# Attention with beacon keys, then a maxout FFN: batch 0 divided at query 512, and the first two batches in a new order

## The chip, the cores and the metric

The kernel runs on one core of a Trainium2 chip. The metric is the device time of one execution in microseconds (us). A core has a matrix engine (TensorE, PE in the profile; its weight loads are PEld), a vector engine (VectorE, DVE), an engine for functions and copies (ScalarE, ACT), a general engine (GpSimd, POOL) and a queue engine (SyncE, SP). Each works through its own instructions in order; they wait for one another by semaphores. Transfers between the main memory and the on-chip memory (SBUF) are DMAs, issued here by SP, ACT and POOL. Matrix products are accumulated in PSUM, a small memory of eight banks of 512 fp32 columns.

## The reference

Inputs are q, k and v (8 batches, 8 heads, 576 positions, 64 features), 16 beacon keys and values per head, three input weights (512 x 768) and an output weight (768 x 512), all fp32. Per batch and head:

```python
k_all = concatenate([beacon_k, k]); v_all = concatenate([beacon_v, v])   # 592 keys
scores = q @ k_all.T / sqrt(64)          # causal among the 576; beacons seen by all
a = exp(scores - max); a /= sum(a)
x = a @ v_all                            # then heads side by side: 4608 tokens x 512
h = maximum(maximum(x @ w1, x @ w2), x @ w3)
out = h @ w_out                          # 4608 x 512
```

## The kernel before, in words

Work is cut into 16 quads: quad Q is batch Q // 2 and four of its eight heads. For a quad the four heads lie on four groups of 32 partitions, and each pair of features is one 32-bit word. q and k come in (fp32 for quads 0 and 1, cast in a separate instruction; bf16 by a casting DMA of POOL for all later ones), and VectorE turns them with 32 x 32 transposes of words into `qT` and `kT` (`turn`, L197 to L205). The beacon keys go through `turn_first_beacon_k` (L160) or `turn_beacon_k` (L148) and `put_beacon_k` (L167).

Keys are in five tiles of up to 128, tile 0 beginning with the 16 beacons. Tile t needs only queries from `q_min[t]` on (0, 112, 240, 368, 496), so a quad has 576 + 464 + 336 + 208 + 80 = 1664 columns of scores per head. They are cut into steps of at most 512 columns (`bursts`, L69 to L87): four steps of their own shape for each of quads 0 to 3, and full 512-column steps running across quads from quad 4 on. A step (`emit_scores`, L258) is a run of small matmuls into two PSUM tiles of two heads each, then two exponentials on ScalarE (L288), one per tile, which write bf16 probabilities to `at_sb`; no maximum is subtracted. `emit_masks` (L298) zeroes the causal triangle with POOL selects (L304).

The division by the sum comes afterwards. For quads 0 to 3 `pv_pass` (L316) makes, for each half of the queries (288), three passes: part 0 multiplies the probabilities by ones and gets the sums, from which ScalarE makes a logarithm (L344) and an exponential of its negative (L346), that is the reciprocal; parts 1 and 2 multiply by the even and odd columns of v, and VectorE multiplies PSUM by the reciprocal into `xT` (L350). From quad 4 on `pv_segment` (L357) does the three parts together, for queries 0 to 239 and then 240 to 575. `xT` is a ring of four batches, already transposed for the FFN.

The FFN runs in nine blocks of 512 tokens. A block is 18 first-layer units (`mm1_unit`, L427: four 512-column matmuls; the first of three results is copied to `hT`, by ScalarE, or for block 0 by VectorE at L447, the others are joined by a maximum on VectorE, L449) and four second-layer units (`mm2_unit`, L451: six matmuls, a copy, an output DMA). Units are taken strictly in order, and one may start when the last batch that its tokens reach is complete (`ready`). Block 0 takes all of w1 first, then w2, then w3.

The order is written by hand (`tc.manual_schedule()`): every engine executes what `emit_all` (L606) emits, in that order. `begin` (L544) starts 17 multiplications of zeros (`spare`, L538) and the first loads: SP issues the k of quad 0 in two pieces, its q in two, the k and q of quad 1 (L183), beacon keys, v of batch 0 (L218) and the small beacon loads. Then come the steps in order. Around them stand probability passes, `heads` (transposes between a step's two exponentials), FFN units up to a running allowance (2 per step in steps 8 to 15, then 2.6 and 3.4), and `plan`, work tied to a step (`at_step`, L565 to L579): the loads of later quads and of the weights on POOL's queue, the casts of v, the transposes. FFN units begin behind step 8, when both quads of batch 0 have been divided. After the last step the rest of the units run.

```python
N_APART = 2 * n_quad
by_burst = [
    [[(0, 0, HALF), (3, q_min[3], S)], [(1, q_min[1], S)], [(2, q_min[2], S)]]
    + [[(0, HALF, S), (4, q_min[4], S)]],
    [[(t, q_min[t], S) for t in range(n_kt)]],
]
```

Of the kernel before, what the change touches and what calls it, by code (L numbers as in the profile page):

```python
# [16 lines left out]
def kernel(  # L17
# [27 lines left out]
    HG = 4  # L45
# [15 lines left out]

    BANK = 512
    N_APART = 2 * n_quad
    by_burst = [
        [[(0, 0, HALF), (3, q_min[3], S)], [(1, q_min[1], S)], [(2, q_min[2], S)]]
        + [[(0, HALF, S), (4, q_min[4], S)]],
        [[(t, q_min[t], S) for t in range(n_kt)]],
    ]
    bursts = []  # L69
    at_piece = {}  # L70
    for Q in range(NQ):
        apart = Q < N_APART
        pos = 0
        if Q <= N_APART:
            room = 0
        for group in by_burst[0 if apart else 1]:
            if apart:
                room = 0
            for t, q0, q1 in group:
                at_piece.setdefault((Q, t), []).append((q0, q1, pos))  # L80
# [7 lines left out]
    AT_W = pos  # L88
# [4 lines left out]
    RING = 4  # L93
# [8 lines left out]
    st_pool = ctx.enter_context(tc.tile_pool(name="st", bufs=4))  # L102
    vst_pool = ctx.enter_context(tc.tile_pool(name="vst", bufs=2))
# [3 lines left out]
    nrm_pool = ctx.enter_context(tc.tile_pool(name="nrm", bufs=2))  # L107
    ffn_h = ctx.enter_context(tc.tile_pool(name="ffn_h", bufs=2))
# [29 lines left out]
    for x in first32:  # L138
        nc.gpsimd.memset(x, 0.0)
# [38 lines left out]
    def load_qk(Q, which, cuts):  # L178
        st = st_pool.tile([128, QS * D], FP32, name="st")
        stage[Q, which] = st  # L180
        for s0, s1 in zip(cuts, cuts[1:]):
            cols = slice(s0 * D, s1 * D)
            nc.sync.dma_start(out=st[:, cols], in_=qk_rows(Q, which)[:, cols])  # L183
# [5 lines left out]
    def cast_qk(Q, which, cast, s0=0, s1=QS):  # L189
# [4 lines left out]
        if s1 == QS:  # L194
            stage.pop((Q, which))

    def turn(Q, which, s0=0, s1=QS):  # L197
# [6 lines left out]
        if s1 == QS:  # L204
            stage.pop((Q, which, 16))  # L205
# [3 lines left out]
    def load_v(b, queue=None):  # L209
        queue = queue or nc.sync  # L210
# [3 lines left out]
        for t in range(n_kt):  # L214
# [43 lines left out]
    def emit_scores(k):  # L258
# [6 lines left out]
        for heads in ((0, 1), (2, 3)) if burst[0][0] < n_quad else (range(HG),):  # L265
# [50 lines left out]
    def pv_pass(Q, hf, part):  # L316
        b, g = divmod(Q, n_quad)
        at_sb, v_sb = at[Q], v_tiles[b]
        h0, h1 = hf * HALF, (hf + 1) * HALF
# [6 lines left out]
        ps = pv_pool[0].tile([128, HALF], FP32, name="pv")  # L326
# [15 lines left out]
        if part == 0:  # L342
            lnd = nrm_pool.tile([128, S - SPLIT], FP32, name="lnd")[:, 0:HALF]
            nc.scalar.activation(out=lnd, in_=ps, func=AF.Ln)  # L344
            recip = nrm_pool.tile([128, S - SPLIT], FP32, name="recip")[:, 0:HALF]
            nc.scalar.activation(out=recip, in_=lnd, func=AF.Exp, scale=-1.0)  # L346
            recips[Q, hf] = recip
        else:
            c0 = b % RING * S + h0
            nc.vector.tensor_mul(xT[:, 2 * g + part - 1, c0 : c0 + HALF], ps, recips[Q, hf])  # L350
# [6 lines left out]
    def pv_segment(Q, seg):  # L357
# [8 lines left out]
        pv_banks = pv_pool[1].tile([128, 2 * BANK], FP32, name="pv2")  # L366
# [28 lines left out]
        recip = nrm_pool.tile([128, S - SPLIT], FP32, name="recip")[:, 0:n]  # L395
# [13 lines left out]

    def pv_pairs(Q):  # L410
        if Q >= N_APART:
            return [[(Q, 0)], [(Q, 1)]]
        return [
            [(Q, 0, 0), (Q, 1, 0)],
            [(Q, 0, 1), (Q, 0, 2)],
            [(Q, 1, 1), (Q, 1, 2)],
        ]

    def emit_pv(passes):
        if len(passes) == 1:  # L420
            return pv_segment(*passes[0])
        for one in passes:
            pv_pass(*one)

    hTs = {}

    def mm1_unit(tb, ft, i, pool, name):  # L427
# [15 lines left out]
        if i == 0 and tb > 0:  # L443
            nc.scalar.copy(hT[:, ft, :], ps)  # L444
        elif i == 0:

            nc.vector.tensor_copy(hT[:, ft, :], ps)  # L447
        else:
            nc.vector.tensor_max(hT[:, ft, :], hT[:, ft, :], ps)  # L449
# [68 lines left out]

    plan = {}
# [199 lines left out]
```

## Time and profile before

| what | value |
|---|---|
| median of 3 runs (lowest, highest) | 287.39 us (287.2, 287.74) |
| the profiled execution, its span | 287.24 us, 285.5 us |
| busy: PE, DVE, ACT, POOL | 272.4, 171.2, 157.5, 88.9 us |
| mean granted PE clock over the span | 0.981 |
| first FFN weight load | 29.36 us into the span |
| first scores of quad 4 (step 16) | 54.44 us |
| DMA, moved and mean rate | 33.08 MB, 116 GB/s |

The span is the time from the first to the last profiled instruction of the program. Busy time of an engine is the union of its instructions; matmuls overlap in a pipeline, so a PE that counts as busy may still be waiting in part. In the lines shown below, "x16" counts instructions, what stands behind "<-" in brackets is what ended the idle time ahead of them, and a name ending in q (SPq, POOLq) is an engine's instruction queue. The 40 slices of the page are each a fortieth of the span, about 7.1 us, and a digit is a tenth.

### The profile page before, as it was taken

The numbers are of one execution on the slowest core, as the hardware profiler recorded it, in microseconds if no ns is written. First come the engines' busy times: TensorE is split into PE (matmuls) and PEld (weight loads), VectorE is DVE, ScalarE is ACT, GpSimd is POOL, SyncE is SP. The second block draws the span as 40 slices with busy tenths as digits, with TensorE's granted clock in tenths as the row PEclk, the third lists the DMA queues.
The fourth block names the chain that finished last, engine by engine and source line by source line (L and its number), as shares of the span: only waits on it lengthen the run. The fifth ranks groups of instructions, "written<-read, shape, count | busy, mean of one in ns | idle before, by whom it ended". The sixth has DMA issues, their size and how long they took to land.

```text
span 285.5 us, 8144 instructions
## 1 busy us (share of the span) xinstructions
PE 272.4 (95%) x3469; PEld 140.2 (49%) x3503; DVE 171.2 (60%) x298; ACT 157.5 (55%) x246; POOL 88.9 (31%) x165
## 2 busy tenths in 40 slices
PE   7597999999999999999999999999999999999995
PEld 2235444534545454445456877445454554444442
DVE  3717769856675766656657575666544454554553
ACT  5798576457784766557664686376647620210210
POOL 0484862235553523152415340442134100000000
PEclk9859999999999999999999999999999999999999
DMA  7899999689964954159046913490031003003004
GB/s 246 226 181 209 144 186 205 94 151 238 203 114 123 218 103 84 48 164 195 5 83 197 203 22 69 152 170 2 2 112 39 2 0 131 18 0 147 3 0 147
DMA packets 51924, 33.08 MB, mean 116 GB/s; under 512 B 41264, under 2 KB 42288, under 8 KB 51888
## 3 DMA queue, kind: packets, MB, share of 16 engines
q1 hardware_dynamic: 41152, 20.40, 27.0%
q0 software_dynamic: 10464, 12.01, 26.5%
q8 instruction: 27, 0.44, 0.6%
q10 hardware_dynamic: 272, 0.15, 0.2%
q14 instruction: 9, 0.07, 0.1%
HBM read 35.13 MB, written 9.44 MB: 156 GB/s over the span
## 4 chain that ended last, share of the span: by engine, by line
PE 90%; ACT 4%; DMA 2%; DVE 1%; issue 1%; SPq 0%; DVEq 0%
PE fps L436 37%; PE fps L456 11%; PE sc L273 11%; PE pv L385 10%; PE pv L436 7%; PE sc L436 6%; ACT at_sb L288 3%; PE pv L334 3%; PE sc L456 2%; PE pv L456 2%; DMA st<-in_q_dram 2%; DVE qT L200 1%; DVE xT L350 0%; ACT recip L346 0%; SPq L183 0%
## 5 line engine op out<-in xcount | busy, mean ns | idle before, releaser
L288 ACT ACTIVATE at_sb<-sc 128x1024 bf16<-128x1024 f32 (+7 forms) x128 | 104.0, 861 | 31.8 <-PE sc L273 31.5
L436 PE MATMUL fps<-xT,w_sb 128*128 128x512 bf16 (+1 forms) x507 | 115.0, 358 | 2.2 <-issue 1.3
L436 PEld LDWEIGHTS <-w_sb 128*128 128x128 bf16 x720 | 66.9, 98 | 68.8 <-issue 7.2
L304 POOL TENSOR_SCALAR_AFFINE_SELECT at_sb<-at_sb 128x512 bf16<-128x512 bf16 (+6 forms) x89 | 48.0, 556 | 126.9 <-ACT at_sb L288 121.8
L449 DVE TENSOR_TENSOR hT<-hT,fps 128x512 bf16<-128x512 bf16 x80 | 54.7, 685 | 33.2 <-PE fps L436 27.3
L273 PE MATMUL sc<-qT,kT 32*128 32x288 bf16 (+15 forms) x960 | 40.1, 266 | 4.5 <-DVE qT L200 2.1
L444 ACT CAST hT<-fps 128x512 bf16<-128x512 f32 x34 | 19.9, 586 | 30.1 <-PE fps L436 30.1
L401 DVE TENSOR_TENSOR xT<-pv,recip 128x240 bf16<-128x240 f32 (+1 forms) x48 | 19.7, 453 | 28.0 <-ACT recip L396 27.5
L456 PE MATMUL fps<-w_out_sb,hT 128*128 128x512 bf16 x144 | 34.9, 379 | 0.5 <-issue 0.3
L456 PEld LDWEIGHTS <-hT 128*128 128x128 bf16 x210 | 19.8, 98 | 25.4 <-DVE hT L449 1.7
L273 PEld LDWEIGHTS <-kT 32*128 32x128 bf16 x960 | 19.1, 94 | 24.1 <-issue 18.0
L394 ACT ACTIVATE lnd<-pv 128x240 f32<-128x240 f32 (+1 forms) x24 | 9.9, 412 | 31.1 <-PE pv L385 31.0
L464 DVE COPY y<-fps 128x512 f32<-128x512 f32 x25 | 17.3, 692 | 12.6 <-PE fps L456 12.2
L200 DVE STREAM_TRANSPOSE kT<-c 128x256 uint32<-128x256 uint32 (+1 forms) x32 | 22.0, 708 | 3.5 <-ACT c L193 3.5
L436 PE MATMUL pv<-xT,w_sb 128*128 128x512 bf16 (+1 forms) x107 | 22.4, 339 | 0.1
L200 DVE STREAM_TRANSPOSE qT<-c 128x256 uint32<-128x256 uint32 (+1 forms) x32 | 21.5, 701 | 0.3 <-ACT c L193 0.3
L385 PE MATMUL pv<-at_sb,v_sb 128*32 128x160 bf16 (+7 forms) x864 | 21.5, 242 | 0.0
L436 PE MATMUL sc<-xT,w_sb 128*128 128x512 bf16 x78 | 20.3, 379 | 0.1
L385 PEld LDWEIGHTS <-v_sb 128*32 128x32 bf16 (+1 forms) x864 | 16.3, 96 | 1.3
L226 POOL CAST v_sb<-vst 128x1024 bf16<-128x1024 f32 (+1 forms) x18 | 15.7, 894 | 0.8 <-issue 0.8
L449 DVE TENSOR_TENSOR hT<-hT,pv 128x512 bf16<-128x512 bf16 x15 | 10.3, 688 | 7.6 <-PE pv L436 4.1
L449 DVE TENSOR_TENSOR hT<-hT,sc 128x512 bf16<-128x512 bf16 x13 | 8.9, 688 | 7.4 <-PE sc L436 5.5
(50 smaller groups left out, 146.9 us busy)
## 6 DMA issues: line engine op xcount, KB each, us to landing
out_dram<-y SPq DMA_DIRECT2D x35, 256.0 KB, 2.0
vst<-in_v_dram SPq DMA_DIRECT2D x21, 256.0 KB, 5.2
c<-in_k_dram POOLq DMA_DIRECT2D x14, 288.0 KB, 5.4
c<-in_q_dram POOLq DMA_DIRECT2D x14, 288.0 KB, 6.7
w_sb<-in_moe_w_dram POOLq DMA_DIRECT2D x3, 768.0 KB, 8.4
vst<-in_v_dram SPq DMA_DIRECT2D x7, 224.0 KB, 3.9
vst<-in_v_dram SPq DMA_DIRECT2D x7, 160.0 KB, 7.6
w_out_sb<-in_moe_w_out_dram POOLq DMA_DIRECT2D x1, 768.0 KB, 9.6
```

The source lines that it names most:

```text
L200: nc.vector.transpose(dst.rearrange("p (t s) -> p s t", s=RUN)[:, s0:s1], src.rearrange("p (s d) -> p s d", d=DP),)
L226: cast(v_tiles[b][0:n, t0:t1].rearrange("p t h d -> p (t h d)"), stage["v", b][0:n, t0:t1].rearrange("p t h d -> p (t h d)"),)
L273: nc.tensor.matmul(sc[h // 2][:, h % 2, off : off + w], kT[hs, 128 * t : 128 * (t + 1), j], qT[hs, q0:q1, j], start=(j == 0), stop=(j == 1 ...
L288: nc.scalar.activation(out=at[Q][:, 2 * i : 2 * i + 2, a0 : a0 + w], in_=sc[i][:, :, off : off + w], func=AF.Exp, scale=scale,)
L304: nc.gpsimd.affine_select(out=view, in_=view, compare_op=ALU.is_ge, fill=0.0, base=q0 - (128 * t - Nb), pattern=[[0, HG], [1, edge - q0]], ...
L385: nc.tensor.matmul(pv_banks[32 * j : 32 * j + 32, c : c + w], lhsT, at_sb[0:r, j, a : a + w], start=(t == 0), stop=all(x[1] // BANK != c / ...
L401: nc.vector.tensor_mul(xT[:, 2 * g + part - 1, c0 : c0 + n], pv_banks[:, offs[part] : offs[part] + n], recip,)
L436: nc.tensor.matmul(ps[:, o0 : o0 + n], w_in[i][:, ct, 128 * ft : 128 * (ft + 1)], xT[:, ct, x0 : x0 + n], start=(ct == 0), stop=(ct == n_c ...
L444: nc.scalar.copy(hT[:, ft, :], ps)
L449: nc.vector.tensor_max(hT[:, ft, :], hT[:, ft, :], ps)
L456: nc.tensor.matmul(ps, hT[:, ft, 128 * tt : 128 * (tt + 1)], w_out_sb[:, ft, :], start=(ft == 0), stop=(ft == n_ft - 1),)
L464: nc.vector.tensor_copy(y, ps)
```

## The change

1. The score steps of the first two quads. Queries 0 to 511 of batch 0 (`main`) are made first, in three steps per quad (0 to 5); then queries 512 to 575 of both quads (`rest`), and then quads 2 and 3 whole, run together in full steps (6 to 13). Quad 4 begins at step 14. There are 53 steps in place of 55.
2. Dividing. `pv_pass` of batch 0 covers queries 0 to 287 and 288 to 511. The remaining 64 queries of both quads are done by one `pv_rest`: 120 matmuls of 64 columns into one bank, one logarithm, one exponential, two multiplies. Quads 2 and 3 use `pv_segment`. Block 0 of the FFN, tokens 0 to 511, thus needs only the main part.
3. Loads of quad 0. q and k come in halves of 288 tokens, each in four DMAs, one per head on 32 partitions (`load_half`): the first k half from SP and ACT, the first q half from SP, ACT and POOL, the second k half from SP, the second q half as bf16 from POOL (`load_half16`). The beacon keys of quad 0 are issued by POOL instead of ACT. The first k half is cast by VectorE, the first q half by POOL, the second k half by ScalarE. The memory for them is cleared by VectorE instead of POOL.
4. Zeros. 30 multiplications of 256 columns in place of 17 of 512 before the first scores, and 36 more of them between the early steps.
5. The order. `plan` and the allowance of the early steps give way to one list, `orders`, walked up to step 13. In it S is a step with its first exponential, E the second exponential and the masks, s, p, r, g and h are probability work, C casts, t transposes, B and b beacon keys, k, w, v loads, c casts of v, x zeros, f one FFN unit (with 1, its copy by VectorE; with 2, in the pool of the probability passes). By step 14, 21 units have been emitted and quads 0 to 3 are divided.
6. Later. The rate is 3.2 units per step in place of 3.4, `xT` holds all eight batches, the reciprocals have a pool of four, v's staging has one buffer, and the very last `pv_segment` uses a score tile instead of the one that the segment ahead of it uses.

The core of the diff:

```diff
+    main = [[(0, 0, HALF), (1, q_min[1], HALF)]]
+    main.append([(2, q_min[2], HALF), (0, HALF, TOKB), (1, HALF, TOKB)])
+    main.append([(2, HALF, TOKB), (3, q_min[3], TOKB), (4, q_min[4], TOKB)])
+    rest = [[(t, TOKB, S) for t in range(n_kt)]]
+    whole = [[(t, q_min[t], S) for t in range(n_kt)]]
...
+    order = [(Q, main) for Q in range(n_quad)] + [(Q, rest) for Q in range(n_quad)]
+    order += [(Q, whole) for Q in range(n_quad, NQ)]
...
-    RING = 4
+    RING = B
...
+    def load_half(which, half, queues):
+        st = half_pool.tile([128, HRUN * D], FP32, name="half32")
+        stage[0, which, half] = st
+        for h in range(HG):
+            src = (q, k)[which][0, h, HALF * half : HALF * (half + 1)]
+            queues[h % len(queues)].dma_start(
+                out=st[32 * h : 32 * h + 32], in_=src.rearrange("(p s) d -> p (s d)", s=HRUN)
+            )
...
+    def pv_rest():
+        n_r = S - TOKB
+        bank = pv_pool[0].tile([128, 512], FP32, name="pv")
+        ps = bank[:, 0 : 3 * n_quad * n_r].rearrange("p (g c n) -> p g c n", g=n_quad, c=3)
+        for part in range(3):
+            for Q in range(n_quad):
+                for t in range(n_kt):
+                    a = next(a + TOKB - q0 for q0, q1, a in at_piece[Q, t] if q0 <= TOKB < q1)
...
+                        nc.tensor.matmul(
+                            ps[32 * j : 32 * j + 32, Q, part],
+                            lhsT,
+                            at[Q][0:n, j, a : a + n_r],
...
+        for part in (1, 2):
+            nc.vector.tensor_mul(
+                xT[:, part - 1 : n_ct : 2, TOKB:S], ps[:, :, part], recip
+            )
...
     def spare(n):
-
         ps = ffn_psum.tile([128, TOKB], FP32, name="fps")
         for _ in range(n):
-            nc.tensor.matmul(ps, zeros[:, 0:128], zeros, start=True, stop=True)
+            nc.tensor.matmul(ps[:, 0:256], zeros[:, 0:128], zeros[:, 0:256], start=True, stop=True)
...
     def begin():
-        spare(17)
-        load_first_beacon_k(0, nc.scalar)
-        load_qk(0, 1, (0, SH, QS))
-        load_qk(0, 0, (0, SH, QS))
-        load_qk(1, 1, (0, QS))
-        load_qk(1, 0, (0, QS))
+        load_half(1, 0, (nc.sync, nc.scalar))
+        load_half(0, 0, (nc.sync, nc.scalar, nc.sync, nc.gpsimd))
+        load_first_beacon_k(0, nc.gpsimd)
+        load_half16(0, 1)
+        load_half(1, 1, (nc.sync,))
+        load_qk(1, 1)
         load_first_beacon_k(1, nc.sync)
+        load_qk(1, 0)
         load_v(0)
         load_beacon_k(1, 2, nc.sync)
+        load_beacon_k(2, B, nc.sync)
...
+        orders = (
+            "C 0 1 1 0; C 0 0 0 2; C 0 1 0 1; t 0 1 0; B 0; t 0 0 0; x 29; k 2 0; x 1; t 0 1 1; t 0 0 "
+            "1; S 0; C 1 0 2 2; x 4; E 0; S 1; x 3; x 2; B 1; x 4; C 1 1 2 1; t 1 1 0; x 4; t 1 1 1; "
+            "E 1; t 1 0 0; x 2; S 2; E 2; t 1 0 1; k 2 1; w 0; c 0 2; x 6; s 0 0; t 2 0 0; S 3; x 6; "
+            "x 3; E 3; S 4; E 4; x 2; c 2 4; c 4 5; s 0 1; p 0 1 1; S 5; p 0 0 2; p 0 1 2; k 3 1; E "
+            "5; v 1 0 1; s 1 0; w 1; k 3 0; p 0 0 1; b 2; v 1 1 2; S 6; b 3; p 1 0 2; p 1 0 1; s 1 1; "
+            "t 2 1 1; p 1 1 1; E 6; v 1 2 3; p 1 1 2; t 2 0 1; f; f 2; t 2 1 0; t 3 1 1; S 7; b 4; f "
+            "1; E 7; f 2; r; w 2; f 1 2; v 1 3 4; S 8; t 3 0 1; t 3 0 0; E 8; f 1; v 1 4 5; f; f 1 2; "
+            "S 9; f 2; E 9; t 3 1 0; f; w 3; g 2 0; S 10; f 1; E 10; h 2 0; f; f 1; S 11; E 11; f 1; "
+            "f 1; f 1; k 5 1; k 4 0; S 12; E 12; g 2 1; k 4 1; S 13; E 13; h 2 1; f; f; k 5 0; g 3 0; "
+            "t 4 0 1; t 4 0 0; h 3 0; f; t 4 1 1; f; g 3 1; t 4 1 0; f; h 3 1 "
+        )
...
-        first_rate, rate = 2.6, 3.4
+        first_rate, rate = 2.6, 3.2
...
+        first, second = segs
+        emit_ffn(len(units), B - 2)
+        finish = pv_segment(*first)
+        banks = sc_psum.tile([128, 2, BANK], FP32, name="sc").rearrange("p a n -> p (a n)")
+        finish_second = pv_segment(*second, banks)
+        finish()
+        finish_second()
+        emit_ffn(len(units), B - 2)
```

334 lines of the change are left out of this document (186 added, 148 removed).

## The prediction

> **What bounds the kernel now.** I read the page's slices first, then the stages, then the order of time in the first stage.
>
> ```profile
> PE 272.4 (95%) x3469; PEld 140.2 (49%) x3503; DVE 171.2 (60%) x298; ACT 157.5 (55%) x246; POOL 88.9 (31%) x165
> PE   7597999999999999999999999999999999999995
> PEclk9859999999999999999999999999999999999999
> DMA  7899999689964954159046913490031003003004
> ```
>
> TensorE (PE) is the bound from the fifth slice on; only the first four, some 28 us, are in question, and there the granted clock dips as well. The stages:
>
> ```profile
> 8.00:16.00 8.00, 5.68 (x56) 2.28 (x56) 4.89 (x11) 6.58 (x8) 4.75 (x7) 0.73 0.91 201
> 16.00:24.00 8.00, 7.44 (x123) 3.70 (x123) 3.21 (x8) 7.54 (x12) 6.17 (x10) 0.63 1.06 189
> 24.00:32.00 8.00, 6.38 (x157) 3.90 (x145) 5.69 (x12) 4.00 (x8) 4.18 (x7) 1.00 1.17 191
> ```
>
> The columns are PE, PEld, DVE, ACT, POOL busy, granted clock, DMA share, GB/s. From 8 to 24 us ScalarE (ACT) is the full engine (6.58 and 7.54 of 8 us), and PE's "busy" there is scores waiting on it. In order of time:
>
> ```profile
> 0.81 0.84 SPq L183 DMA_DIRECT2D st<-in_k_dram  x2
> 1.48 5.46 PE L542 MATMUL fps<-zeros 128*128 128x512 bf16 x17 [1.48 <-DVE zeros L536]
> 4.78 0.33 SPq L183 DMA_DIRECT2D st<-in_q_dram  x1
> 5.22 2.03 SPq L158 DMA_DIRECT2D first<-in_beacon_k_dram  x4
> 9.19 6.79 ACT L288 ACTIVATE at_sb<-sc 128x992 bf16<-128x992 f32 x8 [1.66 <-PE sc L273]
> 10.81 1.14 POOL L193 CAST c<-st 128x1152 bf16<-128x1152 f32 x1 [9.77 <-DMA st<-in_q_dram]
> 16.23 1.89 ACT L288 ACTIVATE at_sb<-sc 128x992 bf16<-128x992 f32 x2 [0.26 <-PE sc L273]
> 19.06 1.58 PE L334 MATMUL pv<-at_sb,ones 128*32 128x288 bf16 x32
> 20.01 0.41 ACT L344 ACTIVATE lnd<-pv 128x288 f32<-128x288 f32 x1
> 20.45 0.45 ACT L346 ACTIVATE recip<-lnd 128x288 f32<-128x288 f32 x1
> 21.57 2.76 ACT L288 ACTIVATE at_sb<-sc 128x672 bf16<-128x672 f32 x4
> 21.99 0.82 DVE L350 TENSOR_TENSOR xT<-pv,recip 128x288 bf16<-128x288 f32 x2 [4.72 <-PE pv L334]
> 29.25 1.17 POOL L304 TENSOR_SCALAR_AFFINE_SELECT at_sb<-at_sb 128x448 bf16<-128x448 bf16 x2 [3.82 <-ACT at_sb L288]
> 29.36 1.41 PEld L436 LDWEIGHTS <-w_sb 128*128 128x128 bf16 x8
> 31.82 1.78 ACT L288 ACTIVATE at_sb<-sc 128x928 bf16<-128x928 f32 x2 [2.63 <-PE sc L273]
> ```
>
> Exponentials of quads 0 and 1 run from 9.19 to 24.33; the first FFN unit stands at 29.36, because it needs all of batch 0. I call that moment F. From F on PE is full:
>
> ```profile
> 40.54 0.90 PE L334 MATMUL pv<-at_sb,ones 128*32 128x288 bf16 x32
> 43.72 0.63 PE L334 MATMUL pv<-at_sb,v_sb 128*32 128x288 bf16 x24
> 46.62 1.18 PE L334 MATMUL pv<-at_sb,v_sb 128*32 128x288 bf16 x40
> 54.44 0.63 PE L273 MATMUL sc<-qT,kT 32*128 32x512 bf16 x8
> 57.70 0.64 PE L273 MATMUL sc<-qT,kT 32*128 32x64 bf16 x16
> ```
> ```profile
> 85.96 1.80 PE pv L385 x76
> 91.02 1.29 PE pv L456 x6
> 93.85 0.86 PE pv L436 x4
> 95.58 0.65 PE pv L385 x24
> ```
> ```profile
> 62.00:231.00 169.00, 166.76 (x2522) 90.84 (x2529) 102.94 (x175) 108.54 (x173) 59.54 (x111) 1.00 0.50 111
> ```
>
> Between F and 54.44 (quad 4's first scores) lie 18 first-layer units of 0.86, seven score steps of about 0.6 and two quads of probability passes (0.90 + 0.63 + 1.18, twice): 15.6 + 4.2 + 5.4 = 25.2, against 25.1 passed. So PE work after F is paid at its own length, and the later stage (166.76 of 169 us) leaves nothing to win. What the change can move is F, and what PE does just behind it.
>
> **The change, part by part.** The sum is made against the profiled execution: 287.24 us, of which 285.5 are span and 1.7 lie around it; the median of the runs is 0.15 above.
>
> *Work dropped from before F.* With token block 0 needing queries 0 to 511 only, quads 0 and 1 want 1344 of their 1664 score columns before F, so ACT does 2 x 2 x 2 x 320 = 2560 columns fewer there: at 1.78 per 2 x 928, 2.5 us. But step 6 (the first of the rest) stands ahead of the last sums in ACT's order with one of its two tiles, 1.0 back.
>
> *The start.* Quad 0 needs only two half loads before its first scores, so these come earlier than 8.54. What holds them is POOL: its cast of the q half stands behind nine DMA issues at about 0.55 (row below), so free at 0.8 + 5.0 = 5.8; cast 0.6, transpose 0.7, scores near 7.3. I bank nothing: the next quad decides.
>
> ```profile
> 36.06 0.58 POOL L187 DMA_DIRECT2D c<-in_k_dram  x1
> st<-in_k_dram SPq DMA_DIRECT2D x1, 576.0 KB, 4.9
> st<-in_q_dram SPq DMA_DIRECT2D x1, 576.0 KB, 6.0
> DMA to landing us min/median/max: 4.0/6.4/11.3
> DMA to landing us min/median/max: 7.9/8.4/10.2
> ```
>
> (The last two are the bf16 q and k loads, L187, and the weights, L249.) Quad 1's q was the sixth issue of SP, at 4.78, and landed at 10.8. Now 13 issues precede it: 9 x 0.42 + 4 x 0.51 + 0.81 = 6.6. With a landing of 4.9 to 6.0 it is there at 11.5 to 12.6; I take 12.1.
>
> *The chain to F.* POOL casts that q (1.14: 13.25), and only behind it come the masks of steps 0 and 1 (1.17 + 0.3: 14.7). The sums of quad 0 wait for those masks, and step 3's scores are queued behind the sums on PE: 0.35 for PE, 0.41 + 0.45 on ACT: 15.95. Then ACT's order is step 3 (1.78), step 4 (1.89), logarithm and reciprocal (0.67), step 5 (1.47), again (0.86), the half of step 6 (1.0), again (0.67): 8.4; seven hand-overs at about 0.15, with 0.26 the one seen, add 1.0: 25.35. Two multiplies of 224 columns (0.82 for two of 288) give F = 26.0, 3.4 earlier.
>
> *Behind F.* Up to quad 4's first scores (step 14) PE now does 18 units of 0.86, 3 second-layer units of 1.29, seven score steps at 0.6, quads 2 and 3 by segments (2 x (0.65 + 1.80) = 4.9, before 5.4), and the rest of batch 0: 120 narrow matmuls. Narrow ones cost by columns (16 with 64 and 448 columns took 0.64, 8 of 512 took 0.63), so 30 groups of four at 64 columns are 1.2. Sum 15.5 + 3.9 + 4.2 + 4.9 + 1.2 = 29.7; step 14 at 55.7. Before, the same state (quads 0 to 3, 21 units) is 54.44 + 3.9 = 58.3. Gain 2.6. All that follows is the same work: 39 score steps, 12 quads, 177 units. The rates 3.4 to 3.2 only move units into the last stage; zero on a full PE. The last segment in its own banks removes at most the 0.4 of one hand-over; I take 0.
>
> *New waits behind F.* Weights and quad 4's loads are issued by POOL behind masks. w1 goes out near 25.0 (step 5's masks end at 23.6, two v issues) and is wanted by the seventh unit, at 26.0 + 5.2 + 1.2 + 1.2 = 33.6; landing 7.9 to 10.2 means 32.9 to 35.2. A wait of 0 to 1.6, and for all loads 0 to 4 (below); nearest is w1's median, no wait, and I take 0.4 over all of them.
>
> *Zeros.* 30 of half width before the scores replace 17 of full width (5.46), so end near 6.2, ahead of the scores. 36 more stand between the early steps, 0.1 each, in time that PE spends waiting on ACT: nothing; without that cover 3.6 us, spread over five gaps, of which the wait for quad 1 alone covers most.
>
> What they may buy is the clock: 32 sums took 1.58 at 19.06 in a stage of granted 0.63, and 0.90 later. [...]
>
> Sum: 287.24 - 2.6 + 0.4 = 285.0, beside the median 285.1.
>
> **Rivals.** *Earlier still.* If quad 1's q is there by about 10.8 as before and ACT never pauses, it needs from 8.0: 5.1 for steps 0 to 2, 0.86, 8.4, the multiplies 0.7 and 0.3 of hand-overs, F = 23.4, 2.6 better: 282.4. For it: ACT was nearly gapless in 9 to 24 us. Against: thirteen issues ahead, and masks behind the cast.
>
> *The start gains nothing.* Quad 1 waits for bytes. Before, 2.36 MB took until 10.8, 3.8 us per MB from 1.8; now quad 2's q (0.59 MB) is requested ahead of quad 1's, 13.0; if q lands 2.5 us past my value, at 14.6, F is 28.5 and the time 287.2. For it: a DMA share of 0.91 already in 8 to 16 us. [...] Against: this chain has few bytes more than before.
>
> *Slower: quad 4's loads late.* Before they were issued at 36.06, 18 us ahead of use. Now q4 is issued behind step 11's masks, near 45.5, and k4 behind step 12's, near 47; their transposes stand on DVE between PSUM evacuations, so a late load stops the FFN too, and step 14 wants them at 55.7. With 6.4 to landing k4 is turned by 54.9: hidden. With 11.3 it is 59.8: a wait of 4.1 on PE, no gain left from 9.9 on, and the time 287.24 - 2.6 + 4.1 = 288.7. For it: the DMA is full (0.9 and more) through 50 us in the slices above. Against: the weights, most of that traffic, are through by 47.
>
> **How the numbers follow.** Forecast 0.48 (own range 283.6 to 286.7); earlier still 0.14; gains nothing 0.14; slower 0.24. A measurement of this kernel tells about 0.2%, 0.57 us, from no change. Faster: 0.48 + 0.14 = 0.62; same 0.14; slower 0.24. Range 282.4 to 288.7, the outer rivals' times.
>
> **What would show it.** Right: first FFN weights load near 26; granted clock 1.0 through 8 to 24 us; POOL's cast of quad 1's q starting near 12.1; step 14's scores near 56; no PE wait over 1 us between. Wrong: that cast past 14; PE waiting on w1 near 33, or on a transpose of quad 4 past 50; the stage from 60 to 230 longer than before; zeros found on the chain between scores.

## The result: slower, and where the profile says so

The changed kernel takes 296.52 us (median of six runs, 294.83 to 296.85), the kernel before, on the same chip, 287.49. The ratio is 1.0291, with an interval of 1.0268 to 1.0313. The forecast was 285.1 with a range of 282.4 to 288.7; the time lies outside it.

The page of the changed kernel, profiled at 296.37 us, first the span, then busy times and the slices:

```profile
span 294.7 us, 8667 instructions
PE 274.7 (93%) x3715; PEld 141.5 (48%) x3752; DVE 168.7 (57%) x300; ACT 157.6 (53%) x250; POOL 94.9 (32%) x178
PE   7647979999989899999999999999999999999995
PEclk9989799999999999999999999999999999999999
DMA  6959997975970979531955494128012002102003
```

PE's busy time has grown by 2.3 us, the span by 9.2. From the seventh slice on PE is full nearly throughout, so the loss is early again. The stages (columns as in the prediction: PE, PEld, DVE, ACT, POOL busy, granted clock, DMA share, GB/s):

```profile
8.00:16.00 8.00, 5.14 (x89) 3.86 (x88) 3.72 (x8) 5.59 (x7) 0.09 (x1) 1.00 0.94 201
16.00:24.00 8.00, 5.42 (x95) 3.35 (x98) 3.37 (x6) 3.42 (x5) 6.86 (x11) 0.79 0.68 132
24.00:32.00 8.00, 5.65 (x217) 4.69 (x209) 3.63 (x10) 4.97 (x11) 5.72 (x11) 0.86 1.12 181
```

From 16 to 24 us ACT, the full engine of this stage before (7.54 of 8 us), works 3.42. POOL does next to nothing before 16 (0.09, before 4.75) and is nearly full after it (6.86). The granted clock is 1.00 in the first stage, where it was 0.73, and then dips later, to 0.79 and 0.86. In order of time (the views of the timeline):

```profile
6.58 0.56 POOL L232 DMA_DIRECT2D c<-in_q_dram  x1
7.05 0.42 SPq L228 DMA_DIRECT2D st<-in_q_dram  x1
7.91 0.62 PE L314 MATMUL sc<-qT,kT 32*128 32x288 bf16 x16 [0.76 <-DVE qT L222]
15.91 1.15 POOL L238 CAST c<-st 128x1152 bf16<-128x1152 f32 x1 [8.77 <-DMA st<-in_q_dram]
17.09 3.23 POOL L345 TENSOR_SCALAR_AFFINE_SELECT at_sb<-at_sb 128x448 bf16<-128x448 bf16 x6
17.73 0.31 PE L375 MATMUL pv<-at_sb,ones 128*32 128x288 bf16 x4 [2.88 <-POOL at_sb L345]
19.85 0.44 ACT L387 ACTIVATE recip<-lnd 128x288 f32<-128x288 f32 x1
20.02 2.10 PE L597 MATMUL fps<-xT 128*128 128x256 bf16 x9
20.20 1.76 ACT L329 ACTIVATE at_sb<-sc 128x928 bf16<-128x928 f32 x2
22.06 1.07 PE L314 MATMUL sc<-qT,kT 32*128 32x48 bf16 x24
23.11 1.89 ACT L329 ACTIVATE at_sb<-sc 128x992 bf16<-128x992 f32 x2 [1.15 <-PE sc L314]
29.51 0.30 PE L314 MATMUL sc<-qT,kT 32*128 32x64 bf16 x15 [1.39 <-issue]
33.42 0.81 PE L498 MATMUL fps<-xT,w_sb 128*128 128x512 bf16 x3 [0.16 <-issue]
40.26 0.21 PE L408 MATMUL pv<-at_sb,v_sb 80*32 80x64 bf16 x3 [1.70 <-issue]
41.94 1.90 PE L498 MATMUL fps<-xT,w_sb 128*128 128x512 bf16 x8
65.75 0.63 PE L314 MATMUL sc<-qT,kT 32*128 32x512 bf16 x8
```

Quad 1's q, issued by SP at 7.05, is only cast at 15.91. Quad 0's masks stand behind that cast, its sums behind the masks (PE waits 2.88 us), and the first reciprocal ends at 20.29. The first FFN unit, F, stands at 33.42 (its first weight load, by which the prediction counts F, is at 33.19; one matmul has no record) and step 14 at 65.75. The state that before would have had step 14 at 58.3, by the prediction's estimate, is thus 7.45 us later. Behind step 14 pass 228.9 us (294.7 - 65.75) in place of 227.2: 1.75 more, in which PE shows two waits:

```profile
82.36 1.04 POOL L267 CAST v_sb<-vst 128x1024 bf16<-128x1024 f32 x1 [3.53 <-DMA vst<-in_v_dram]
83.45 0.50 PE L462 MATMUL pv<-at_sb,v_sb 128*32 128x240 bf16 x16 [1.18 <-POOL v_sb L267]
102.25 2.08 PE L498 MATMUL fps<-xT,w_sb 128*128 128x512 bf16 x8 [0.72 <-DVE xT L478]
```

7.45 and 1.75 are the 9.2 us. Here and below, places in time come from one profiled execution of each kernel, ratios from all its runs.

### The profile page after: what moved, and what is told of

Read it like the earlier page. It is cut to its first block, busy times and chain, and to the rows that moved or that the text cites. A ratio compares the mean times of both kernels' runs of the same rounds, so it can differ in the third digit from the quotient of the medians.

```text
span 294.7 us, 8667 instructions
## 1 busy us (share of the span) xinstructions
PE 274.7 (93%) x3715; PEld 141.5 (48%) x3752; DVE 168.7 (57%) x300; ACT 157.6 (53%) x250; POOL 94.9 (32%) x178
## 4 chain that ended last, share of the span: by engine, by line
PE 82%; DMA 8%; issue 3%; ACT 2%; DVE 2%; POOL 1%; SPq 1%; POOLq 0%; DVEq 0%
PE fps L498 31%; PE fps L517 12%; PE pv L462 10%; PE sc L314 9%; PE pv L498 7%; PE sc L498 6%; DMA vst<-in_v_dram 4%; DMA st<-in_q_dram 3%; PE sc L517 2%; PE pv L375 1%; PE pv L517 1%; ACT at_sb L329 1%; DMA half<-in_q_dram 1%; PE fps L597 1%; POOL at_sb L345 1%
## 5 line engine op out<-in xcount | busy, mean ns | idle before, releaser
L498 PE MATMUL fps<-xT,w_sb 128*128 128x512 bf16 x419 | 106.9, 380 | 2.8 <-issue 1.3
L498 PEld LDWEIGHTS <-w_sb 128*128 128x128 bf16 x648 | 60.1, 98 | 75.9 <-issue 8.7
L345 POOL TENSOR_SCALAR_AFFINE_SELECT at_sb<-at_sb 128x512 bf16<-128x512 bf16 (+8 forms) x94 | 48.7, 536 | 124.6 <-ACT at_sb L329 121.6
L478 DVE TENSOR_TENSOR xT<-pv,recip 128x240 bf16<-128x240 f32 (+1 forms) x54 | 22.1, 450 | 32.2 <-ACT recip L473 32.1
L314 PE MATMUL sc<-qT,kT 32*128 32x80 bf16 (+21 forms) x1104 | 36.1, 248 | 4.3 <-issue 1.4
L517 PE MATMUL fps<-w_out_sb,hT 128*128 128x512 bf16 x155 | 37.6, 380 | 0.4 <-issue 0.2
L517 PEld LDWEIGHTS <-hT 128*128 128x128 bf16 x210 | 19.6, 98 | 24.5 <-DVE hT L510 1.4
L498 PE MATMUL pv<-xT,w_sb 128*128 128x512 bf16 x113 | 29.6, 379 | 0.3
L525 DVE COPY y<-fps 128x512 f32<-128x512 f32 x27 | 18.6, 690 | 13.6 <-PE fps L517 13.3
L462 PE MATMUL pv<-at_sb,v_sb 128*32 128x160 bf16 (+7 forms) x952 | 23.8, 243 | 1.2 <-POOL v_sb L267 1.2
L462 PEld LDWEIGHTS <-v_sb 128*32 128x32 bf16 (+1 forms) x1008 | 19.1, 96 | 2.9 <-POOL v_sb L267 1.4
L267 POOL CAST v_sb<-vst 128x1024 bf16<-128x1024 f32 (+1 forms) x18 | 15.9, 908 | 3.5 <-DMA vst<-in_v_dram 3.5
L510 DVE TENSOR_TENSOR hT<-hT,sc 128x512 bf16<-128x512 bf16 x15 | 10.3, 687 | 8.9 <-PE sc L498 8.1
L462 PE MATMUL pv<-at_sb,ones 128*32 128x336 bf16 (+4 forms) x372 | 14.4, 268 | 0.0
```

The lines of the kernel that those rows point to most:

```text
L267: cast(v_tiles[b][0:n, t0:t1].rearrange("p t h d -> p (t h d)"), stage["v", b][0:n, t0:t1].rearrange("p t h d -> p (t h d)"),)
L314: nc.tensor.matmul(sc[h // 2][:, h % 2, off : off + w], kT[hs, 128 * t : 128 * (t + 1), j], qT[hs, q0:q1, j], start=(j == 0), stop=(j == 1 ...
L345: nc.gpsimd.affine_select(out=view, in_=view, compare_op=ALU.is_ge, fill=0.0, base=q0 - (128 * t - Nb), pattern=[[0, HG], [1, edge - q0]], ...
L462: nc.tensor.matmul(pv_banks[32 * j : 32 * j + 32, c : c + w], lhsT, at_sb[0:r, j, a : a + w], start=(t == 0), stop=all(x[1] // BANK != c / ...
L478: nc.vector.tensor_mul(xT[:, 2 * g + part - 1, c0 : c0 + n], pv_banks[:, offs[part] : offs[part] + n], recip,)
L498: nc.tensor.matmul(ps[:, o0 : o0 + n], w_in[i][:, ct, 128 * ft : 128 * (ft + 1)], xT[:, ct, x0 : x0 + n], start=(ct == 0), stop=(ct == n_c ...
```

## The experiments

**First theory: one late transfer.** In the first theory quad 1's q is late because quad 2's q is read ahead of it and because beacon loads stand ahead of it in SP's queue, and F is late with it. Rivals: the zeros, v's single staging buffer, and PE's own instruction supply. Four kernels, each with one part undone.

*e_q2late*, where quad 2's q load stands behind the masks of step 2:

```diff
-t 0 0 0; x 29; k 2 0; x 1; t 0 1 1
+t 0 0 0; x 30; t 0 1 1
...
-t 1 0 1; k 2 1; w 0; c 0 2; x 6; s 0 0; t 2 0 0; S 3
+t 1 0 1; k 2 1; k 2 0; w 0; c 0 2; x 6; s 0 0; S 3
...
-p 1 1 2; t 2 0 1; f; f 2
+p 1 1 2; t 2 0 1; t 2 0 0; f; f 2
```

> The load of quad 2's q moves from behind the cast of quad 0's q to behind the masks of step 2, where quad 2's k is loaded. Shared engines: if that transfer (issued at 6.58 us, landed 9.0 us later) is what holds quad 1's q, that q lands near 12.5 to 13 us in place of 15.9, the first FFN unit comes about 3 us before 33.4, and the time is about 293.5 us against 296.4 of the changed kernel. Issue time on SP: if q lands late because it is the fourteenth issue, at 7.05 us, it still lands past 15 us and the time stays within 0.6 us of 296.4.

Measured 295.82 us, ratio 1.0278 (1.0217 to 1.0339). The timeline of this kernel, PE only, with F in the second row:

```profile
26.75 0.30 PE L314 MATMUL sc<-qT,kT 32*128 32x64 bf16 x15 [2.23 <-issue]
30.42 1.04 PE L498 MATMUL fps<-xT,w_sb 128*128 128x512 bf16 x4 [0.82 <-DMA w_sb<-in_moe_w_dram]
39.42 0.24 PE L408 MATMUL pv<-at_sb,v_sb 80*32 80x64 bf16 x3 [3.23 <-issue]
39.59 1.89 PE L498 MATMUL pv<-xT,w_sb 128*128 128x512 bf16 x4
42.39 1.94 PE L498 MATMUL fps<-xT,w_sb 128*128 128x512 bf16 x8
```

The cast of quad 1's q starts at 11.93, four us earlier, the first reciprocal ends at 17.97 and F stands at 30.42, three us earlier. Step 14 is at 66.23 all the same. F itself still stands behind a longer "issue" wait (2.23 for 1.39) and a wait for the first weights (0.82). Behind F the second "issue" wait is 1.53 longer, and the granted clock, at half from 39.1 to 42.5, costs 1.29 more: from the end of that wait to the unit at 42.39 pass 2.97 us, in the changed kernel 1.68 (40.26 to 41.94). What F gains isn't paid out.

*e_q1first*, where quad 1's q is issued ahead of quad 1's beacon keys:

```diff
+        load_qk(1, 0)
         load_first_beacon_k(1, nc.sync)
-        load_qk(1, 0)
```

> SP issues quad 1's q directly behind quad 1's k, ahead of the four small beacon loads, so near 5.2 us instead of 7.05. Issue time on SP: quad 1's q lands about 1.8 us earlier, near 14 us, and the time falls by about 1.8 to 294.6 us. Shared engines: the engines are full already, the q lands less than 0.7 us earlier, and the time stays within 0.7 us of 296.4.

Measured 296.08 us, ratio 1.0277 (1.0247 to 1.0306). The q is cast at 12.11, but now quad 0's second q half is late: the last of its four loads lands at 11.88, in the changed kernel at 10.23. VectorE stands idle for it, and PE waits for VectorE. It is issued as early as there (5.38 and 5.49), but now behind quad 1's q (5.11).

```profile
11.90 0.70 DVE L222 STREAM_TRANSPOSE qT<-h 128x288 uint32<-128x288 uint32 x1 [3.43 <-DMA h<-in_q_dram]
12.65 1.04 PE L314 MATMUL sc<-qT,kT 32*128 32x224 bf16 x20 [3.07 <-DVE qT L222]
```

The first reciprocal ends at 19.41, F at 32.01. Either edit brings q to 12 us, and neither brings time.

*e_nozeros*, without the 36 zeros between the early steps (every "x" behind "S 0" is taken out of the list):

```diff
-S 0; C 1 0 2 2; x 4; E 0; S 1; x 3; x 2; B 1; x 4; C 1 1 2 1; t 1 1 0; x 4; t 1 1 1
+S 0; C 1 0 2 2; E 0; S 1; B 1; C 1 1 2 1; t 1 1 0; t 1 1 1
...
-t 1 0 0; x 2; S 2; E 2; t 1 0 1; k 2 1; w 0; c 0 2; x 6; s 0 0; t 2 0 0; S 3; x 6
+t 1 0 0; S 2; E 2; t 1 0 1; k 2 1; w 0; c 0 2; s 0 0; t 2 0 0; S 3
...
-x 3; E 3; S 4; E 4; x 2; c 2 4
+E 3; S 4; E 4; c 2 4
```

> The 36 zeros between the steps are gone, the 30 before them stay. Zeros cost: nine of them took 2.10 us at 20.02 us, ahead of step 4's scores, with ScalarE idle for 1.15 us; without them step 4 comes about 1.2 us earlier and the time falls by 1.0 to 1.5 us, to about 295.2. Zeros pay by the clock: without them the clock is granted at half from about 10 us on, the pieces of PE before the first FFN unit grow by over 1 us, and the time is 297 us or more.

Measured 293.85 us, ratio 1.0199 (1.0167 to 1.0232): 0.92% better than the changed kernel, 2.6 us. Its stages, same columns:

```profile
8.00:16.00 8.00, 3.55 (x64) 2.76 (x64) 3.96 (x9) 5.23 (x7) 0.99 (x1) 0.72 1.05 236
16.00:24.00 8.00, 5.50 (x96) 3.51 (x97) 3.59 (x6) 5.30 (x9) 6.46 (x13) 0.50 0.75 139
24.00:32.00 8.00, 4.83 (x220) 4.11 (x220) 3.85 (x10) 4.17 (x10) 5.27 (x10) 0.92 1.19 168
```

PE runs at half clock from 11.6 to 25.2 us, 13.6 us, and the kernel is still faster. The dips of the changed kernel, 19.6 to 23.0 and 29.8 to 33.2, are 3.4 us each, 6.8 us in all; before the change there was one, from 11.6 to 21.9. In the 3.4 us ahead of them PE was busy for 0.98 and 1.75 us, before the change for 1.72; what starts a dip is not shown. With the zeros the time at half clock is shorter, but here they cost more than they buy. One cost is seen: they stand in PE's order ahead of scores for which ACT waits, as the nine at 20.02 do ahead of step 4's (ACT idle 1.15, without them 0.26). How the rest of the 2.6 us comes about is not shown. In the profiled executions F comes earlier by about as much as quad 1's q (cast at 15.01, 0.9 earlier, though the code up to there is the same), the first "issue" wait is 2.76 and the second is gone, and about half of the gain lies behind step 14, where PE doesn't wait for v.

*e_vst2*, with two staging buffers for v, paid for by a ring of four batches for `xT`:

```diff
-    RING = B
+    RING = 4
...
-    vst_pool = ctx.enter_context(tc.tile_pool(name="vst", bufs=1))
+    vst_pool = ctx.enter_context(tc.tile_pool(name="vst", bufs=2))
```

> v's staging gets its two buffers back, and xT its ring of four batches (memory has no room for both). One buffer costs: the wait of 1.2 us for the cast of v at 83.45 us and the 0.7 us at 102.25 go, the stage behind step 14 takes 227.2 us in place of 228.95, and the time falls by 1.2 to 1.75 us, to about 295. Full DMA engines instead: the v load is late because other loads run beside it, both waits stay, and the time is within 0.6 us of 296.4.

Measured 296.33 us, ratio 1.028 (1.0234 to 1.0326). The wait for v stays (0.96 us at 83.1), and behind step 14 still pass 228.84 us. The single buffer isn't the cause of the 1.75 us.

**Second theory: the narrow work behind F.** After e_q2late the new theory is that the 64-query remainder costs the gain: step 6 on ACT ahead of F, and the 120 narrow matmuls, in which PE uses up instructions faster than they come in.

*e_s6late* (step 6 behind the first two units) and *e_rsplit* (the 120 matmuls in three lots of 40, FFN units between):

```diff
-v 1 1 2; S 6; b 3; p 1 0 2; p 1 0 1; s 1 1; t 2 1 1; p 1 1 1; E 6; v 1 2 3; p 1 1 2; t 2 0 1; f; f 2; t 2 1 0; t 3 1 1; S 7; b 4; f 1
+v 1 1 2; p 1 0 2; p 1 0 1; s 1 1; t 2 1 1; p 1 1 1; v 1 2 3; p 1 1 2; t 2 0 1; f; f 2; S 6; b 3; t 2 1 0; E 6; t 3 1 1; f 1; S 7; b 4
```
```diff
-f 2; r; w 2; f 1 2; v 1 3 4
+f 2; r 0; w 2; f 1; r 1; f 1; r 2; v 1 3 4
```

> Step 6 (the rest of batch 0, 64 matmuls of 64 columns) moves from ahead of the last sums of batch 0 to behind the first two FFN units; the number of FFN units and matmuls is the same. Instruction loads: the wait of 1.4 to 4.3 us that the profile ends by nothing it shows, inside step 6, no longer stands ahead of the first FFN unit, and neither does half of step 6's work on ScalarE; that unit comes 2.5 to 4 us earlier, near 30 us, and the time falls by 1.5 to 3 us to about 294, less if the wait comes back behind it. Transfers alone: the unit comes at most 1 us earlier and the time stays within 0.8 us of 296.4.

> The 120 narrow matmuls of the rest of batch 0 run in three lots of 40, with one FFN unit between the lots, in place of all at once; count and shapes are unchanged. Instruction loads: the wait of 1.7 to 3.2 us inside them (1.70 at 40.26 us in the changed kernel) is gone or under 0.3 us, since each FFN unit leaves 0.86 us in which only 8 instructions are used; the time falls by 1.2 to 2 us, to about 294.8. If that wait is something of its own (PSUM, masks), it stays at 1.5 us or more and the time stays within 0.6 us of 296.4.

e_s6late took 296.66 us, ratio 1.0319 (1.0277 to 1.036), e_rsplit 296.37, ratio 1.0294 (1.0254 to 1.0334): neither gains. In e_s6late's profiled execution, its shortest (293.9), F stands at 28.09, where q was cast at 12.79 (the code up to there is that of the changed kernel, so that landing differs by 3 us between executions), and step 14 follows 35.2 us later, at 63.32: step 7 waits 0.78 for ACT, and the second half-clock stretch comes at 27.4 to 30.8. In e_rsplit the "issue" wait inside the 120 is gone (0.92 for POOL's masks stands there), but the earlier one has grown from 1.39 to 3.99.

*e_comb1* puts e_q2late, e_nozeros, e_s6late and e_rsplit together.

> Four edits at once: quad 2's q loaded later, no zeros between steps, step 6 behind two FFN units, the rest of batch 0 in three lots. If quad 1's q, the zeros and the instruction loads are the whole loss ahead of step 14, the first FFN unit comes near 26.5 to 28 us, step 14 near 58 us, and the time is 285.5 to 287.5, level with the kernel before. If the waits only move on (to weights or to later instruction loads), step 14 stays past 61 us and the time is 290 or more.

Measured 293.64 us, ratio 1.0199 (1.0132 to 1.0267): no better than e_nozeros alone. F is at 30.87 behind a wait of 2.04 for the first weights, step 14 at 64.89.

*e_burst*, one execution, measures the "issue" wait by itself. On the kernel before, 192 extra zeros of 16 columns run behind step 12, where the DMA engines are full, and again behind step 40, where they are nearly idle:

```diff
+    def narrow(n):
+        ps = ffn_psum.tile([128, TOKB], FP32, name="fps")
+        for _ in range(n):
+            nc.tensor.matmul(ps[:, 0:16], zeros[:, 0:128], zeros[:, 0:16], start=True, stop=True)
...
+            if k in (12, 40):
+                narrow(192)
```

> The kernel before, with 192 extra multiplications of zeros of 16 columns (384 instructions with their weight loads) behind step 12 (DMA engines full) and again behind step 40 (DMA share about a half). Instruction loads behind full DMA engines: a wait of 1 us or more ended by nothing that the profile shows in or just behind the first lot, under 0.5 us for the second; the first lot takes over 1 us longer than the second. Not instruction loads: the two lots take the same time within 0.3 us.

The kernel took 303.39 us. The lots took 4.83 and 4.78 us from first to last start. Only the second was followed by a wait. The windows around both, and the timeline at the second:

```profile
40.00:50.00 10.00, 10.00 (x255) 6.93 (x244) 1.76 (x3) 3.29 (x6) 2.88 (x5) 0.83 1.11 206
170.00:180.00 10.00, 7.87 (x147) 6.05 (x144) 2.28 (x4) 1.88 (x4) 0.00 (x0) 0.83 0.24 49
```
```profile
174.76 0.80 PE L436 MATMUL fps<-xT,w_sb 128*128 128x256 bf16 x3 [2.13 <-issue]
```

With a DMA share of 0.24 PE waits 2.13 us for nothing that the profile shows; with 1.11 it doesn't. So full DMA engines are not the condition, and that part of the theory fell. The use of many instructions in little time remains, though it can't be the whole condition, for the first lot was as fast. The last section has what the traces show beside such waits.

**Third theory: quad 0's new loads, with the zeros and VectorE's order.**

*e_oldload* loads and casts quad 0 as before the change and issues quad 2's loads behind step 1's masks; all else stays:

```diff
-        load_half(1, 0, (nc.sync, nc.scalar))
-        load_half(0, 0, (nc.sync, nc.scalar, nc.sync, nc.gpsimd))
-        load_first_beacon_k(0, nc.gpsimd)
-        load_half16(0, 1)
-        load_half(1, 1, (nc.sync,))
+        load_first_beacon_k(0, nc.scalar)
+        load_qk(0, 1, (0, SH, QS))
+        load_qk(0, 0, (0, SH, QS))
         load_qk(1, 1)
+        load_qk(1, 0)
         load_first_beacon_k(1, nc.sync)
-        load_qk(1, 0)
...
+        spare(30)
+        for which, s0, s1 in ((1, 0, SH), (1, SH, QS), (0, 0, SH), (0, SH, QS)):
+            cast_qk(0, which, by_act, s0, s1)
...
-E 1; t 1 0 0
+E 1; k 2 1; k 2 0; t 1 0 0
```

> The changed kernel with quad 0 loaded, cast and transposed as before (two pieces each by SP, four casts on ScalarE, beacon keys of quad 0 by ScalarE's queue), quad 1's q right behind, and quad 2's loads behind the masks of step 1; division at 512, zeros and order stay. If the new loads are what delays quad 1's q: its cast starts at 10.4 to 11 us in every profile as in the kernel before, not anywhere from 12.8 to 15.9, the first FFN unit comes near 29 us, and the time is 292 to 293.5 us. If the rest of the order sets the end whatever that q does (as when it came at 11.9 and nothing was gained): the time stays within 1 us of 296.4.

Measured 293.5 us, ratio 1.0201 (1.0165 to 1.0237): 0.9% better than the changed kernel, 2.6 us. Quad 1's q is cast at 10.90, F stands at 29.14, step 14 at 62.15.

```profile
10.90 1.14 POOL L239 CAST c<-st 128x1152 bf16<-128x1152 f32 x1 [10.38 <-DMA st<-in_q_dram]
29.14 1.89 PE L499 MATMUL fps<-xT,w_sb 128*128 128x512 bf16 x4
```

*e_oldload_nz* is the same without the 36 zeros.

> The same with the 36 zeros between the steps removed. If the zeros cost their own 1.2 us ahead of step 4 and move the block of instructions that PE waits for: 1.5 to 2.5 us below the same kernel with zeros, so about 290.5. If their cost came only from the late q: within 0.7 us of the same kernel with zeros.

Measured 291.1 us, ratio 1.0128 (1.01 to 1.0155): another 0.73%, 2.1 us. F is where it was (29.06), step 14 at 60.14. What now comes last in the start is a row of VectorE, and behind it PE:

```profile
12.14 0.25 DVE L173 CAST first<-first 128x64 bf16<-128x64 f32 x1 [4.44 <-DMA first<-in_beacon_k_dram]
16.07 0.98 PE L315 MATMUL sc<-qT,kT 32*128 32x288 bf16 x16 [1.32 <-DVE qT L244]
```

Quad 1's beacon keys stand in VectorE's order ahead of quad 1's k; VectorE waits 4.44 us for their DMA while that k lies there from 8.96 on.

*e_oldcomb* adds step 6 late and the 120 matmuls in lots; *e_part6* is the other end, the later settings of the change alone (ring of eight, one v buffer, four reciprocals, rate 3.2, the last segment in a score tile) on the kernel before.

> Loads of quad 0 as before, no zeros between steps, step 6 behind two FFN units, the rest of batch 0 in three lots: all suspected causes ahead of step 14 undone, and what is left of the change is the division at 512, the order and the later settings. If these causes are the loss, the first FFN unit comes near 26 to 27.5 us, step 14 near 59.5, and the time is 286.5 to 289. If the stretch from the first FFN unit to step 14 keeps stretching (35 us when the unit came at 28.1), step 14 stays near 62 and the time is 290 or more.

> The kernel before with the later settings alone: 3.2 units per step, xT for eight batches, four reciprocals, one staging buffer for v, the last segment in a score tile. If these cost the 1.8 us that the stretch behind step 14 is longer in the changed kernel (228.9 against 227.2 us): 288.5 to 289.5 us. If that came from loads shifted against the steps by the new order: 287 to 287.9 us, no difference.

e_oldcomb took 291.59 us, ratio 1.015 (1.0102 to 1.0197), no gain over e_oldload_nz: F at 26.62, step 14 at 62.30, with waits of 1.25 and 0.78 for ACT in step 7 and the clock at half from 32.4 to 35.8. e_part6 took 287.55, ratio 0.9997 (0.9975 to 1.0018): the later settings alone cost nothing.

**What was left, 1.3%.** Three more kernels on e_oldload_nz.

*e_shift* replaces the 30 zeros ahead of the first scores with 94 of 80 columns, so all that follows comes 64 matmuls (128 instructions, each matmul having its weight load) later in PE's stream:

```diff
-        spare(30)
+        ps = ffn_psum.tile([128, TOKB], FP32, name="fps")
+        for _ in range(94):
+            nc.tensor.matmul(ps[:, 0:80], zeros[:, 0:128], zeros[:, 0:80], start=True, stop=True)
```

> Against e_oldload_nz (291.1 us): the 30 zeros of 256 columns ahead of the first scores become 94 of 80 columns, the same column time but 128 more instructions on PE, with nothing else changed. Instruction blocks: the wait of 1.47 us at 27.45 us sits at a fixed count of instructions (the 704th) in every kernel so far, whatever stands there; it moves 64 matmuls earlier, to about 24 us among the passes ahead of step 6, where ScalarE is the bound, and shrinks or hides; the time is 0 to 1.4 us below 291.1 although work is added. If the wait belongs to step 6 or to the passes behind it: it stays at 27 us and the time is 291.1 or more.

Measured 291.65 us, ratio 1.0101 (1.0042 to 1.0161), no difference from e_oldload_nz. Its timeline of PE:

```profile
25.28 0.51 PE L315 MATMUL sc<-qT,kT 32*128 32x64 bf16 x43 [0.30 <-issue]
29.01 0.81 PE L499 MATMUL fps<-xT,w_sb 128*128 128x512 bf16 x3 [0.35 <-issue]
35.48 0.42 PE L409 MATMUL pv<-at_sb,v_sb 128*32 128x64 bf16 x31 [1.57 <-issue]
```

By count of the matmuls recorded ahead of them these waits stand at 351, 479 and 607. In e_oldload_nz the first one stands at 351 too, but in other work, a probability pass:

```profile
27.45 0.20 PE L376 MATMUL pv<-at_sb,v_sb 128*32 128x48 bf16 x3 [1.47 <-issue]
```

They stay at their count and don't follow the code.

*e_b1late* puts the beacon keys behind quad 1's k in VectorE's order; *e_b2* also spreads step 6 and the 120 matmuls between FFN units:

```diff
-S 1; B 1; C 1 1 2 1; t 1 1 0; t 1 1 1; E 1
+S 1; C 1 1 2 1; t 1 1 0; t 1 1 1; B 1; E 1
```
```diff
-f; f 2; t 2 1 0; t 3 1 1; S 7; b 4; f 1; E 7; f 2; r; w 2; f 1 2
+f; f 2; S 6; b 3; t 2 1 0; f 1; E 6; t 3 1 1; f 2; S 7; b 4; f 1; E 7; r 0; w 2; f 1; r 1; r 2
```

> Against e_oldload_nz (291.1 us): VectorE turns quad 1's beacon keys behind quad 1's k, as in the kernel before, no longer ahead of it. There VectorE stood idle 4.44 us until 12.14 us for that small load while quad 1's k was there. Order on VectorE: step 3's scores come at about 14.7 in place of 16.07 us, the first FFN unit 1.0 to 1.4 us earlier, the time 290.0 +- 0.5. If the rest of the chain (sums of quad 0, masks) holds step 3 anyway: less than 0.4 us.

> e_b1late with step 6 and the rest of batch 0 spread between the first six FFN units (never two narrow pieces in a row). If waits at instruction blocks and hand-overs to ScalarE in these narrow pieces are what remains: the first FFN unit near 25 to 26 us, step 14 near 57.5 to 58.5, the time 286 to 288, level with the kernel before or better. If the division at 512 costs by itself: step 14 past 60 and 289.5 us or more.

e_b1late took 289.3 us, ratio 1.0051 (1.0024 to 1.0078): 0.77%, 2.2 us, for one place in an order. Its profiled execution (289.96, against 290.4) shows only a part of that: step 3's scores come 0.83 us earlier and step 6's 0.96, but the "issue" wait is 2.21 in place of 1.47 and F only 0.23 earlier.

```profile
27.22 0.20 PE L376 MATMUL pv<-at_sb,v_sb 128*32 128x48 bf16 x3 [2.21 <-issue]
```

e_b2 took 289.53, ratio 1.0059 (1.0028 to 1.0091). It has no "issue" wait and F at 26.64, and is no faster than e_b1late: its step 14 is at 59.58, 32.9 us behind F. In its windows PE does 524 matmuls where the kernel before, in 22 us, does 312:

```profile
32.00:60.00 28.00, 27.52 (x524) 13.99 (x522) 17.28 (x33) 16.95 (x28) 11.61 (x21) 1.00 0.99 142
```
```profile
32.00:54.00 22.00, 21.79 (x312) 10.51 (x318) 17.86 (x33) 13.96 (x22) 11.58 (x22) 1.00 1.20 165
```

PE is full there: no wait over 0.3 us is left to remove, only more and narrower pieces. No version that ran beats the kernel before.

By the ratios, of the 2.91% the loads of quad 0 (with quad 2's put later) are 0.90, the inner zeros 0.73 (0.92 when taken out first), the beacon keys' place on VectorE 0.77, and 0.51 is left, each of them uncertain by some 0.4. The last half per cent isn't settled. What stands in the traces for it is PE's 32.9 us between F and step 14, and about one more us behind step 14 (228.2 against 227.2).

## Why the prediction was wrong, step by step

- *What bounds the kernel, and where the change acts*: right. PE is full but for the start, and 7.45 of the 9.2 us are lost ahead of step 14.
- *The start*: right in itself, and worth nothing. The first scores were put near 7.3 and stand at 7.91 (before 8.54).
- *"With a landing of 4.9 to 6.0 it is there at 11.5 to 12.6; I take 12.1"*: this is the first step that failed. SP issued that load at 7.05 (6.6 plus the 0.42 of its own was near), but it took 8.8 us to land, not 6.0:

```profile
st<-in_k_dram SPq DMA_DIRECT2D x1, 576.0 KB, 4.9
st<-in_q_dram SPq DMA_DIRECT2D x1, 576.0 KB, 8.8
```

  In the executions with the same code up to there the cast began between 12.8 and 15.9; with the old loads between 10.3 and 11.6. Bringing q alone to 12 us gave no time (e_q2late, e_q1first); undoing the new loads gave 0.9% (e_oldload). The rival "the start gains nothing" had this mechanism, and its 14.6 was near. Its price was too small, because it kept the rest of the sum (and 2.5 us on the forecast of 285.0 are 287.5, not 287.2).
- *The chain to F, 8.4 of ACT, hand-overs of 1.0 and 0.7 of multiplies*: 10.1 from the first reciprocal; it took 13.1 (20.29 to 33.42). The "seven hand-overs at about 0.15" failed: one is 1.15 (behind the nine zeros), and step 6's scores stood 1.39 us in an "issue" wait, a kind of wait that the sum doesn't have at all. Of the 7.2 us by which F missed (33.2 against 26.0) 3.8 lie ahead of the cast, 0.5 between the cast and the first reciprocal, 2.9 in this chain.
- *Zeros "in time that PE spends waiting on ACT: nothing"*: failed, they cost 2.1 to 2.6 us. The bound of 3.6 without cover was the better number. How that divides into scores held up and added "issue" waits is open. The clock that they were to buy pointed the wrong way: without the zeros PE was longer at half clock (13.6 us against 6.8), and the kernel 0.92% faster. That the zeros hold the full clock, no run shows: with them it was 1.00, 0.79 and 0.86 in the three stages.
- *Behind F, 29.7*: it took 32.33. The 120 matmuls were 1.2 "by columns"; from 37.43 to 40.47 they took 3.0, of which 1.70 is one "issue" wait. The 18 units took 16.1 (predicted 15.5; in e_b2, without waits, 16.6), the other terms were within 0.2. The check of these prices on the kernel before, 25.2 against 25.1, came out by luck: there a unit took 0.91 and not 0.86, a score step 0.50 and not 0.6.
- *"All that follows is the same work"*: 1.75 us more, 1.18 of it the wait for v's cast. It is neither v's buffer (e_vst2) nor, on the kernel before, any of the later settings (e_part6).
- *New waits behind F, 0.4*: no wait for weights came, but only because F was late. With F three us earlier the first weights, which the term didn't price, became a wait of 0.8 to 2.0 (e_q2late, e_comb1); with the old loads and F at 26.6 to 29.1 none came.
- *The rival "slower: quad 4's loads late"*: right in sign, wrong in mechanism; nothing waited for quad 4.
- The list of signs did its work: "that cast past 14" and "zeros found on the chain between scores" were named as what would make the forecast wrong, and both came.

Beyond the single terms, the sum itself was too trusting. It moved F and let all behind it follow. The runs show F anywhere from 26.6 to 34.0 with step 14 between 59.6 and 66.2, and twice (e_q2late against the changed kernel, e_oldcomb against e_oldload_nz) an F earlier by 2.4 to 3 us with a step 14 no earlier. A part of this is the clock: in the changed kernel the second stretch at half clock ends where F begins (33.2), in these two it lies behind F, where PE is full (39.1 to 42.5 and 32.4 to 35.8; in e_q2late this cost 1.29 us).

## What to carry to other kernels

A load that the next stage needs is priced from its place behind every small DMA ahead of it, with the slowest landing seen and not the median: here it took 8.8 us, priced at 6.0. When several queues meet at a start, undo one delay at a time and expect no gain: here the next one covered it (e_q2late and e_q1first had q at 12 us and no time from it), and only the time of the run, not an earlier milestone, counts. Filler work is not free where something that another engine waits for stands behind it in the same order: the 36 zeros cost 2.1 to 2.6 us. Cutting matmuls narrower adds instructions, and among the 64 and the 120 narrow ones PE stood 1.39 and 1.70 us in "issue" waits.

## What the runs showed of the hardware

PE stood still for 0.3 to 4.4 us at set places of its instruction stream, whatever work lay there. Counted in recorded matmuls, the first wait came behind 351 of them (with their weight loads 705 instructions) in each of ten kernels: the changed one (1.39), e_q2late (2.23), e_q1first (2.54), e_nozeros (2.76), e_vst2 (4.35), e_rsplit (3.99), e_oldload (1.31), e_oldload_nz (1.47), e_b1late (2.21) and e_shift (0.30). A second came 256 matmuls, that is 512 instructions, later, in the changed kernel (1.70, where one record is missing), e_q2late (3.23), e_q1first (1.58), e_oldload (1.26), e_shift (1.57) and e_s6late (0.26), and in e_shift one half-way between. The wait of e_burst stands at 5057 instructions, which is 705 and 17 times 256. e_s6late, e_comb1, e_oldcomb and e_b2, where the 64 narrow matmuls of step 6 come behind the count of 351, have no "issue" wait there. The kernel before, with 157 matmuls in the busiest of its three stages where the changed one has 217, shows none. The page lists a DMA queue of the kind "instruction" (section 3, packets, MB, share):

```profile
q8 instruction: 29, 0.48, 0.7%
```

Its 29 packets are of 16 KiB, one for every 257 of PE's 7467 recorded matmuls and weight loads (27 in the kernel before, with 6972). The trace keeps the time of each packet. In the changed kernel PE began the 256 instructions ahead of the first wait at 24.24, a packet ran from 27.29 to 28.23, and PE went on at 29.51, 1.28 us behind its end. Ahead of the second wait a packet ran from 37.71 to 38.77, and PE went on at 40.26, 1.49 us behind its end. That "issue" is here a wait for instructions is the author's reading of these counts and times. What sets the time of a packet stays open.

Beside two of the changed kernel's 29 packets PE stood still, for 1.39 and 1.70 us, both times in stretches of many short matmuls (the 64 of step 6 and the 120 of the rest). In e_b2, without such a wait, the kernel took 289.53 us, no less than e_b1late's 289.3 with one of 2.21.
